# Gate and value weights of a fused mixer and two MoE layers: every chunk decoded whole in SBUF, and four low parts made on TensorE

## The chip, the cores and the metric

One core of one Trainium2 chip runs the whole program in one launch. The metric is the device time of one execution in microseconds (us); lower is better. Engines are called as in the profile: PE is TensorE, ACT is ScalarE, DVE is VectorE, POOL is GpSimd, and SP is the queue that issues the DMAs.

## The reference

A recurrent attention runs over 768 steps for 4 batches and 8 heads of 48 dimensions. Its output (3072 tokens of 384 channels) goes through a gated layer and then through a second layer:

```
for t in range(S):
    cur = einsum('bhd,bhe->bhde', u * k[t], v[t])
    y[t] = einsum('bhd,bhde->bhe', r[t], state + cur)
    state = w[t][..., None] * state + einsum('bhd,bhe->bhde', k[t], v[t])
x = y                                        # 3072 x 384
x = (sigmoid(x @ w_gate) * (x @ w_val)) @ w_out    # 384 -> 1536 -> 384
h = x @ w_in                                 # 384 -> 2048
out = (h * tanh(softplus(h))) @ w_out2       # 2048 -> 384
```

All inputs and the output are four-byte floats. The weights arrive as eight-byte integers that hold the four-byte values of two neighbours, seen by the kernel as pairs of 32-bit words.

## The kernel before, in words

**Stages.** The 768 steps are cut into 24 chunks of 32 (`NJ`), taken in 12 pairs `p` (`NP`). For every pair, `fine(p)` makes the products inside small blocks on POOL and, for pair 0, on DVE too (L487), and DVE sums them into the tile `A` (L507). `coarse(p)` transposes r, k and w of the pair on DVE (RD at L601, KD at L605, WD at L612), scales them (L624), and PE multiplies them (the scores `lp`, L643). DVE turns `A` into `X` (L653), and eight **merges** copy parts of `lp` into `X` (L664, three copies each, on ACT or DVE). `keys(p)` updates k on POOL and DVE turns it into `KT` (L696); eight **gathers** on ACT copy it into `KK` (L705). `step(j)` makes the output of a chunk on PE (`yp`, L737), splits it on ACT and DVE into a high and a low f16 part (`xs`, L213 and L216), transposes it (`xp`, L756), and copies it into `xt` (L763, L765). Then it makes the outer products for the state on PE (`kp`, L829), which read `KK`, and joins them to the state (L840).

**The two layers.** Every operand of a large matmul is held as two f16 parts, high and low, and three products are taken. For a pair `p` and each of 12 blocks `f` of 128 columns, `gate` takes nine matmuls for the gate and nine for the value (`gv`, L889), then ACT's sigmoid (L900), DVE's product (L905), ACT's high part (L917) and DVE's low part (L920) go into `gt`. `out1` multiplies `gt` by `wos` (`o`, L957). The second layer follows when all pairs are done.

**Weights of the first layer.** They come in chunks of 256 columns: six for the gate (`wg`), six for the value (`wv`), taken in turn (wg0, wv0, wg1, ...; the number in that order is `count`), then six chunks of the output weights (`wo`). Each chunk is loaded by SP (L268) and decoded: ACT takes out the spare bits (`low_`, L239) and the rebased word (`word_`, L249), DVE **joins** them by a shift and an or, ACT casts the word to f16 (the high part), and the word less the high part is the **low part**. Two ways of decoding exist:

- `decode`, for odd `count` (`WHOLE`), that is the value chunks, and for the output weights: the word lies in SBUF as one tile of 128x768; join L293 on DVE, cast L304 on ACT, low part L307 on POOL or DVE.
- `decode_early`, for even `count`, the gate chunks: the word lies in PSUM as two halves of 128x384 (in the banks `pg3` and `po`, which are free at that time); join L388 and low part L401 on DVE, twice each, and cast L398 on ACT.

**The order of the work** is set by `Plan`: every piece of work is added with its engine (or a cost for each of several engines) and with what it reads and writes, a pass from the end gives each a latest start, and a pass from the start gives every engine the ready piece whose latest start is earliest. The chosen order is then fixed for each engine's queue. Tiles with few buffers limit this order: three for raw chunks (`raw0` to `raw2`), two for words and two for spare bits (`count % 2`), two for `blk`. While pair 0 is in `gate`, its sums rotate over three PSUM banks, later over four.

## Time and profile before

| what | us |
|---|---|
| median of the three timed runs (942.68 to 943.63) | 942.82 |
| the profiled execution, its own time | 939.37 |
| span of that execution in the profile | 937.7 |
| PE busy in it | 874.2 |
| DVE, POOL, ACT busy in it | 661.3, 487.7, 479.1 |

The profile is of one execution on the one core. A line of the source (L293 and so on) is the line of the kernel before. A busy time counts an instruction from its start to its end; two neighbours on one engine overlap by some 0.08 us, so that sums of busy times are a little above the time that passes. A wait is put down to what was seen to come last.

### The profile page before, as it was taken

How to read it: one execution, taken by the hardware profiler on the slowest of the kernel's cores; microseconds unless marked ns; L12 is line 12 of the kernel's file. 1: busy time of each engine (PE TensorE's matmuls, PEld its weight loads, DVE VectorE, ACT ScalarE, POOL GpSimd, SP SyncE). 2: the span in 40 equal slices, each digit the busy share in tenths (PEclk: the TensorE clock that was granted, in tenths of full speed). 3: DMA queues.
4: the chain of work that ended last, by engine and by line, in shares of the span. 5: the costliest groups of instructions: out<-in, count | busy, mean ns of one | idle time of the engine just before them, and what ended most of it. 6: DMA issues, size and time to landing. Idle time of an engine off the chain costs nothing.

```text
span 937.7 us, 29380 instructions
## 1 busy us (share of the span) xinstructions
PE 874.2 (93%) x12808; PEld 703.9 (75%) x12808; DVE 661.3 (71%) x1094; ACT 479.1 (51%) x1065; POOL 487.7 (52%) x528
## 2 busy tenths in 40 slices
PE   0478799999999999999999999999999999999998
PEld 0366678888888888888888886667677676776788
DVE  7999985766785868677688888775655556555541
ACT  2769855352525333342528667675555655556540
POOL 8999931726565464637472275553433434334330
PEclk9989899999999999999999999999999999999999
DMA  9457742213223322232114930010200102000000
GB/s 314 135 166 227 239 119 73 60 47 81 74 60 84 83 56 72 65 85 59 53 47 119 261 102 13 12 40 2 68 1 18 52 1 69 1 19 18 1 34 35
DMA packets 56464, 71.89 MB, mean 77 GB/s; under 512 B 20752, under 2 KB 37648, under 8 KB 56208
## 3 DMA queue, kind: packets, MB, share of 16 engines
q1 hardware_dynamic: 56336, 70.03, 25.3%
q8 instruction: 100, 1.64, 0.8%
q14 instruction: 28, 0.23, 0.1%
HBM read 56.64 MB, written 9.44 MB: 70 GB/s over the span
## 4 chain that ended last, share of the span: by engine, by line
PE 78%; DVE 11%; ACT 5%; DMA 3%; issue 2%; POOL 1%; SPq 0%; ACTq 0%; DVEq 0%; POOLq 0%
PE gv L889 22%; PE h L1067 20%; PE o L1182 18%; PE o L957 13%; PE yp L737 2%; PE kp L829 2%; DVE X L664 1%; ACT X L664 1%; PE lp L643 1%; DMA raw_wp<-wo 1%; ACT KK L705 1%; DVE A L507 1%; DVE KD L605 1%; DVE WD L616 1%; DVE pt L487 1%
## 5 line engine op out<-in xcount | busy, mean ns | idle before, releaser
L1067 PE MATMUL h<-x,wis 128*128 128x512 f16 x864 | 199.9, 379 | 0.0
L889 PE MATMUL gv<-xt,wgs 128*128 128x256 f16 x1296 | 168.8, 277 | 10.5 <-DVE gt L920 7.3
L957 PE MATMUL o<-gt,wos 128*128 128x256 f16 x1296 | 166.9, 274 | 6.4 <-DVE wos L307 2.7
L889 PE MATMUL gv<-xt,wvs 128*128 128x256 f16 x1296 | 166.3, 274 | 1.3 <-DVE gt L920 0.7
L1101 POOL TENSOR_TENSOR sum<-e 128x256 f32<-128x256 f32 x96 | 71.4, 744 | 183.1 <-ACT e L1078 182.9
L487 POOL TENSOR_TENSOR blk<-blk 128x384 f32<-128x384 f32 (+3 forms) x139 | 123.6, 904 | 53.2 <-DMA blk<-rkw 33.7
L889 PEld LDWEIGHTS <-wgs 128*128 128x128 f16 x1296 | 126.5, 99 | 28.9 <-ACT X L664 6.0
L1067 PEld LDWEIGHTS <-wis 128*128 128x128 f16 x864 | 83.5, 98 | 82.9
L957 PEld LDWEIGHTS <-wos 128*128 128x128 f16 x1296 | 125.7, 98 | 25.8 <-DVE wos L307 3.4
L889 PEld LDWEIGHTS <-wvs 128*128 128x128 f16 x1296 | 126.4, 98 | 18.0 <-POOL wvs L307 1.1
L487 POOL TENSOR_TENSOR pt<-blk 128x384 f32<-128x384 f32 x93 | 107.0, 1175 | 50.3 <-DMA blk<-rkw 48.8
L1078 ACT ACTIVATE e<-h 128x512 f32<-128x512 f32 x96 | 57.3, 597 | 84.1 <-PE h L1067 83.2
L900 ACT ACTIVATE sig<-gv 128x512 f32<-128x512 f32 x72 | 43.0, 600 | 86.3 <-PE gv L889 86.0
L917 ACT CAST gt<-gv 128x512 f16<-128x512 f32 x72 | 42.0, 584 | 72.8 <-DVE gv L905 72.6
L1182 PE MATMUL o<-wps,gt 128*128 128x192 f16 x612 | 74.0, 246 | 0.0
L905 DVE SCALAR_TENSOR_TENSOR gv<-gv,sig 128x512 f32<-128x512 f32 x72 | 50.4, 702 | 25.6 <-PE gv L889 20.3
L624 POOL TENSOR_TENSOR RD<-RD,WD 128x256 f32<-128x256 f32 (+2 forms) x32 | 33.6, 1050 | 63.2 <-PE lp L643 32.9
L1120 DVE SCALAR_TENSOR_TENSOR gt<-e,gt 128x256 f16<-128x256 f32 x41 | 27.5, 682 | 49.7 <-ACT gt L1115 49.7
L920 DVE TENSOR_TENSOR gt<-gv,gt 128x512 f16<-128x512 f32 x72 | 49.3, 684 | 16.6 <-ACT gt L917 15.6
L1182 PE MATMUL o<-wps,wgs 128*128 128x192 f16 x498 | 59.4, 246 | 0.0
L664 ACT COPY X<-lp 24x64 f32<-24x64 f32 x159 | 40.7, 256 | 34.1 <-DVE X L664 25.9
L1182 PE MATMUL o<-wps,wos 128*128 128x192 f16 x456 | 57.1, 246 | 0.0
(109 smaller groups left out, 1490.4 us busy)
## 6 DMA issues: line engine op xcount, KB each, us to landing
v<-vt SPq DMA_DIRECT2D x96, 96.0 KB, 2.6
blk<-rkw SPq DMA_DIRECT2D x22, 384.0 KB, 3.8
raw_wi<-wi SPq DMA_DIRECT2D x8, 768.0 KB, 5.1
raw_wp<-wo SPq DMA_DIRECT2D x8, 768.0 KB, 5.8
blk<-rkw SPq DMA_DIRECT2D x11, 512.0 KB, 3.9
raw_wg<-wg SPq DMA_DIRECT2D x6, 768.0 KB, 6.2
raw_wv<-wv SPq DMA_DIRECT2D x6, 768.0 KB, 6.5
raw_wo<-wo SPq DMA_DIRECT2D x6, 768.0 KB, 5.4
```

Source lines behind the costliest of these rows:

```text
L487: engines[e].tensor_tensor(out=pv, in0=a, in1=b, op=ALU.mult)
L664: put(out=xp[p][o : o + t, xs, t:], in_=lps[p, e][i : i + t, :, c : c + C - t])
L889: nc.tensor.matmul(gps[p, i, o][:, h], w[:, a, kc, fs], xt[p][:, c, kc, :], start=(n == 0), stop=(n == 3 * KC - 1),)
L900: nc.scalar.activation(out=sgs[p, i], in_=gps[p, i, 0], func=AF.Sigmoid, scale=1.0 / (SW * SX))
L905: nc.vector.scalar_tensor_tensor(out=gps[p, i, 1], in0=gps[p, i, 1], scalar=SG / (SW * SX), in1=sgs.pop((p, i)), op0=ALU.mult, op1=ALU.mult,)
L917: nc.scalar.copy(out=gt[p][:, 0, 2 * i : 2 * i + 2], in_=gps[p, i, 1])
L920: nc.vector.tensor_tensor(out=gt[p][:, 1, 2 * i : 2 * i + 2], in0=gps[p, i, 1], in1=gt[p][:, 0, 2 * i : 2 * i + 2], op=ALU.subtract,)
L957: nc.tensor.matmul(ops[p, c][:, :NT], wos[:, a, f, cs], gt[p][:, g, f, :], start=(f == 0 and n == 0), stop=(f == NF1 - 1 and n == 2),)
L1067: nc.tensor.matmul(hps[r, f], w2["wi"][:, a, kc, fs], x2[r][:, c, kc, :], start=(n == 0), stop=(n == 3 * KC - 1),)
L1078: nc.scalar.activation(out=es[r, f], in_=hps[r, f], func=AF.Mish, scale=ih)
L1101: engines[e].tensor_tensor(out=sums[0][:, n - 1], in0=a(), in1=b(), op=op)
L1182: nc.tensor.matmul(ops2[h, first], home(slots[r, i, name])[:, c, tsl], w2["wp"][:, a, w, i, :], start=(new and n == 0), stop=(n == 3 * NF2 ...
```

## The change

All twelve gate and value chunks now go through `decode`, with the word whole in SBUF (`WHOLE = range(12)`). For the first four in the order (wg0, wv0, wg1, wv1; `BYPE`) the low part is made elsewhere: PE multiplies a four-byte identity (`eyes[1]`) by half of the word and adds a negative two-byte identity (`eyes[2]`) times the high part, into the PSUM banks `pg3` and `po`, and ACT casts the result to f16. POOL makes the three identities in the place of one. The weights are added to the plan step by step among the gate blocks of pair 0 (`AHEAD`), not all ahead of them, and the second transpose of r now follows the first.

```diff
--- before.py
+++ after.py
@@ -42,7 +42,9 @@
 YPOS = (4, 7)
 SEM = 0.1
 SHARED = (0,)
-WHOLE = range(1, 12, 2)
+WHOLE = range(12)
+BYPE = range(4)
+AHEAD = 2
 COLD = 1.9
 BURST = 1.42
 PARTS = ((), (0,), (1,), (2, 3))
@@ -232,6 +234,7 @@
     raws = {}
     words = {}
     lows = {}
+    rests = {}
 
     def spare_bits(key):
         low = lows[key].rearrange("p a b -> p (a b)")
@@ -269,7 +272,9 @@
 
         add("sp", 2.2, go, reads, [("raw", slot)], lat=2.0)
 
-    def decode(key, dst, n, count, slot, reads, high_on, lo_on, halves=False, blocks=None):
+    def decode(
+        key, dst, n, count, slot, reads, high_on, lo_on, halves=False, blocks=None, by_pe=False
+    ):
 
 
 
@@ -317,7 +322,26 @@
             return
         made = [[(key[0], f, a) for f in blocks or [key[1]]] for a in range(2)]
         add(high_on, 0, high, [word, *reads], made[0])
-        add(lo_on, 0, rest, [word, *made[0]], made[1])
+        if not by_pe:
+            add(lo_on, 0, rest, [word, *made[0]], made[1])
+            return
+        for h in range(2):
+            bank = (("pg", 3), "po")[h]
+            hs = slice(128 * h, 128 * h + 128)
+
+            def differ(e, h=h, hs=hs):
+                pool, tag = ((pg, "pg3"), (po, "po"))[h]
+                t = pool.tile([128, 512], F32, tag=tag, name=f"rest_{name}_{h}")
+                t = rests[key, h] = t[:, : KC * 128].rearrange("p (a b) -> p a b", a=KC)
+                nc.tensor.matmul(t, eyes[1], words[key][:, :, hs], start=True, stop=False)
+                nc.tensor.matmul(t, eyes[2], dst()[:, 0, :, hs], start=False, stop=True)
+
+            def low_part(e, h=h, hs=hs):
+                nc.scalar.copy(out=dst()[:, 1, :, hs], in_=rests.pop((key, h)))
+
+            cold = COLD if key[1] < 2 else 1.0
+            add("pe", 0.85 * cold, differ, ["eye", word, *made[0]], [bank])
+            add("act", 0.48, low_part, [bank], [made[1][h]])
 
     def combine(key, dst, word, low, reads, high_on, lo_on, count):
         sums = {}
@@ -665,7 +689,7 @@
 
         attn("dve", 1.88, flip_k, [K], [KD])
         attn("dve", 1.05, lambda e: flip_r(e, 0), [R], [(*RD, 0), (*RD, 1)])
-        attn("dve", 1.05, lambda e: flip_r(e, 1), [R], [(*RD, 2)])
+        attn("dve", 1.05, lambda e: flip_r(e, 1), [R, (*RD, 0)], [(*RD, 2)])
         attn("dve", 1.3, flip_w, [W], [WD])
         both = {"dve": 0.35, "pool": 0.65}
         attn(both, 0, lambda e: scaled(e, 5, 6, 1, 2), [WD], [(*RD, 2)])
@@ -1242,47 +1266,54 @@
     def unit(e):
 
         first = mp.tile([128, 2, NF1, NT], F16, tag="gt1", name="first")
-        eyes[0] = eye = first[:, 0, 0, :128]
-        nc.gpsimd.memset(eye, 1.0)
-        nc.gpsimd.affine_select(
-            out=eye,
-            in_=eye,
-            pattern=[[1, 128]],
-            base=0,
-            channel_multiplier=-1,
-            compare_op=ALU.is_equal,
-            fill=0.0,
-        )
+        eyes[0] = first[:, 0, 0, :128]
+        eyes[1] = first[:, 0, 1].bitcast(F32)
+        eyes[2] = first[:, 0, 0, 128:]
+        for n, value in enumerate((1.0, 1.0, -1.0)):
+            nc.gpsimd.memset(eyes[n], value)
+            nc.gpsimd.affine_select(
+                out=eyes[n],
+                in_=eyes[n],
+                pattern=[[1, 128]],
+                base=0,
+                channel_multiplier=-1,
+                compare_op=ALU.is_equal,
+                fill=0.0,
+            )
 
     add("act", 1.3, lambda e: nc.scalar.preload_act_table(AF.Sigmoid), [], ["table1"])
     add("dve", 0.2, consts, [], ["consts"])
     attn("dve", 1.3, lambda e: nc.vector.memset(A, 0.0), [], ["A"])
     halves = [("KK", i // 8, i // 4 % 2, i // 2 % 2, i % 2) for i in range(16)]
     attn("pool", 1.8, lambda e: nc.gpsimd.memset(KK, 0.0), [], halves)
-    attn("pool", 0.4, unit, [], ["eye"])
+    attn("pool", 1.5, unit, [], ["eye"])
     attn("sp", 0.1, lambda e: nc.sync.dma_start(out=U, in_=ub), [], ["U"], lat=2.0)
     load_pair(0)
     load_pair(1)
     for j in range(3):
         load_v(j)
 
-    count = 0
-    for i in range(6):
+    def weights(i):
         cs = slice(256 * i, 256 * i + 256)
-        for name, dst, w in (("wg", wgs, wg), ("wv", wvs, wv)):
+        for n, (name, dst, w) in enumerate((("wg", wgs, wg), ("wv", wvs, wv))):
+            count = 2 * i + n
             if count in WHOLE:
                 load_raw((name, i), lambda: dp, in_cols(w, cs), (KC, 256), count % 3)
                 part = lambda dst=dst, cs=cs: dst[:, :, :, cs]
                 both = [2 * i, 2 * i + 1]
-                decode((name, i), part, (KC, 256), count, count % 3, (), W1HI, W1LO, False, both)
+                by_pe = count in BYPE
+                decode(
+                    (name, i), part, (KC, 256), count, count % 3, (), W1HI, W1LO, False, both, by_pe
+                )
             else:
                 decode_early(name, i, dst, in_cols(w, cs), count)
-            count += 1
-    for i in range(6):
-        cs = slice(2 * i, 2 * i + 2)
-        dst = lambda cs=cs: wos[:, :, cs]
-        load_raw(("wo", i), lambda: dp, in_rows(wo1, cs), (2, DM), i % 3)
-        decode(("wo", i), dst, (2, DM), i, i % 3, (), W1HI, W1LO)
+        if i < 5:
+            return
+        for i in range(6):
+            cs = slice(2 * i, 2 * i + 2)
+            dst = lambda cs=cs: wos[:, :, cs]
+            load_raw(("wo", i), lambda: dp, in_rows(wo1, cs), (2, DM), i % 3)
+            decode(("wo", i), dst, (2, DM), i, i % 3, (), W1HI, W1LO)
 
     def tail1(p):
         coarse(p, cells[p])
@@ -1331,6 +1362,10 @@
             if f == 0 and p >= NP - 1:
                 load_x2(0)
                 load_x2(1)
+            if p == 0 and f % 2 == 0:
+                for i in range(AHEAD) if f == 0 else [f // 2 + AHEAD - 1]:
+                    if i < 6:
+                        weights(i)
             if f % 2 == 0:
                 fill, finish = gate(p, f // 2)
             fill(f % 2, 0)
```

Three places show how the queues move. In the names, the number behind a tile's name only tells the buffers of one program apart.

DVE at its first weights, in the middle of pair 0's transposes. Before:

```order
L605 STREAM_TRANSPOSE KD_177<-blk_95 128x32x32
L507 TENSOR_REDUCE A<-pt 128x2x4x4
L388 SCALAR_TENSOR_TENSOR word_wg_148<-word_wg_148,low_wg_143 128x384
L653 STREAM_TRANSPOSE X_257<-A 128x32x32
L401 TENSOR_TENSOR wgs<-word_wg_148,wgs 128x3x128
L664 COPY X_257<-lp_0_189 24x8x8
```

In the changed kernel:

```order
L629 STREAM_TRANSPOSE KD_176<-blk_95 128x32x32
L531 TENSOR_REDUCE A<-pt 128x2x4x4
L298 SCALAR_TENSOR_TENSOR word_wg_154<-word_wg_154,low_wg_147 128x768
L677 STREAM_TRANSPOSE X_252<-A 128x32x32
L298 SCALAR_TENSOR_TENSOR word_wv_167<-word_wv_167,low_wv_159 128x768
L688 COPY X_252<-lp_0_183 24x8x8
```

One join of 768 columns stands for the half of 384, the low part on DVE is gone, and the join of wv0 comes ahead of the merges.

DVE at the end of the decoding, where pair 2 is made ready. Before:

```order
L920 TENSOR_TENSOR gt_784<-gv_5_1_1327,gt_784 128x512
L840 TENSOR_TENSOR s_939<-kp_0_1176,s_939 128x384
L653 STREAM_TRANSPOSE X_1456<-A 128x32x32
L840 TENSOR_TENSOR s_939<-kp_1_1177,s_939 128x384
L293 SCALAR_TENSOR_TENSOR word_wo_1471<-word_wo_1471,low_wo_1432 128x768
L696 STREAM_TRANSPOSE KT<-blk_335 128x24x32
L905 SCALAR_TENSOR_TENSOR gv_0_1_1420<-gv_0_1_1420,sig 128x512
L905 SCALAR_TENSOR_TENSOR gv_1_1_1475<-gv_1_1_1475,sig 128x512
L601 STREAM_TRANSPOSE RD_1600<-blk_670 128x2x8x32
L664 COPY X_1456<-lp_0_1531 24x8x8
```

In the changed kernel:

```order
L677 STREAM_TRANSPOSE X_1558<-A 128x32x32
L298 SCALAR_TENSOR_TENSOR word_wo_1560<-word_wo_1560,low_wo_1523 128x768
L944 TENSOR_TENSOR gt_711<-gv_5_1_1322,gt_711 128x512
L688 COPY X_1558<-lp_0_1436 24x8x8
L688 COPY X_1558<-lp_0_1436 16x8x16
L688 COPY X_1558<-lp_0_1436 8x8x24
L688 COPY X_1558<-lp_0_1436 24x8x8
L688 COPY X_1558<-lp_0_1436 16x8x16
L688 COPY X_1558<-lp_0_1436 8x8x24
L864 TENSOR_TENSOR s_993<-kp_1_1248,s_993 128x384
L720 STREAM_TRANSPOSE KT<-blk_355 128x24x32
L929 SCALAR_TENSOR_TENSOR gv_0_1_1509<-gv_0_1_1509,sig 128x512
```

DVE's merges for pair 2, two of them in place of four, now come ahead of the transpose KT.

ACT at the same place. Before:

```order
L705 COPY KK<-KT 32x16x24 x2
L664 COPY X_1456<-lp_0_1531 24x8x8
L664 COPY X_1456<-lp_0_1531 16x8x16
L664 COPY X_1456<-lp_0_1531 8x8x24
L664 COPY X_1456<-lp_0_1531 24x8x8
```

In the changed kernel:

```order
L688 COPY X_1558<-lp_1_1437 24x8x8
L688 COPY X_1558<-lp_1_1437 16x8x16
L688 COPY X_1558<-lp_1_1437 8x8x24
L729 COPY KK<-KT 32x16x24
L729 COPY KK<-KT 32x16x24
L215 ACTIVATE xs_1060<-yp_0_1664 128x192
L729 COPY KK<-KT 32x16x24 x6
```

Before, two gathers stand ahead of ACT's four merges and six behind; now all eight stand behind ACT's six merges.

## Rows read from the trace of the kernel before

**Rows 1.** Busy time by stretch: each engine's us (and instructions), TensorE clock, DMA.
```profile
0.00:23.40 23.40, 0.00 (x0) 0.00 (x0) 17.70 (x22) 4.91 (x6) 18.98 (x21) 1.00 0.94 314
23.40:49.00 25.60, 13.47 (x461) 9.97 (x461) 23.80 (x40) 18.24 (x43) 24.17 (x24) 1.00 0.44 145
49.00:126.50 77.50, 60.61 (x1208) 48.21 (x1205) 72.57 (x106) 61.88 (x118) 68.54 (x59) 0.89 0.61 192
126.50:140.00 13.50, 13.47 (x292) 11.86 (x292) 13.35 (x20) 5.07 (x10) 4.66 (x6) 1.00 0.60 152
```
**Rows 2.** PE's waits from 23.4 to 126.6 us: total us, times, longest us.
```profile
PE gv L889 <- DVE gt L920: 7.3, 2, 5.9
...
PE o L957 <- DVE wos L307: 2.7, 2, 2.5
...
PE o L957 <- ACT wos L304: 1.9, 1, 1.9
```
**Rows 3.** Timeline of PE: start us, us, engine, line, out<-in, count [idle before].
```profile
48.99 2.10 PE L889 MATMUL gv<-xt,wgs 128*128 128x256 f16 x9
...
125.25 1.27 PE L829 MATMUL kp<-v,KK 32*64 32x48 f32 x60 [0.95 <-DVE xs L216]
```
**Rows 4.** Timeline of DVE and ACT where pair 2 is made ready.
```profile
112.57 2.10 DVE L696 STREAM_TRANSPOSE KT<-blk 128x768 f32<-128x768 f32 x1
116.35 0.83 ACT L664 COPY X<-lp 24x64 f32<-24x64 f32 x3 [0.52 <-PE lp L643]
119.04 1.94 DVE L664 COPY X<-lp 24x64 f32<-24x64 f32 x6 [0.90 <-ACT X L664]
...
121.86 2.07 ACT L705 COPY KK<-KT 32x384 f32<-32x384 f32 x4
123.96 0.33 ACT L213 ACTIVATE xs<-yp 128x192 f16<-128x192 f32 x1
124.31 1.03 ACT L705 COPY KK<-KT 32x384 f32<-32x384 f32 x2
```
**Rows 5.** DVE's groups, 0 to 130 us, by shape: count | busy us, mean ns | idle.
```profile
L293 DVE SCALAR_TENSOR_TENSOR word_wv<-word_wv,low_wv 128x768 uint32<-128x768 uint32 x6 | 7.3, 1219 | 0.1
L388 DVE SCALAR_TENSOR_TENSOR word_wg<-word_wg,low_wg 128x384 uint32<-128x384 uint32 x12 | 6.6, 551 | 0.3 <-ACT word_wg L249 0.3
L401 DVE TENSOR_TENSOR wgs<-word_wg,wgs 128x384 f16<-128x384 f32 x12 | 6.5, 544 | 0.0
...
L307 DVE TENSOR_TENSOR wos<-word_wo,wos 128x768 f16<-128x768 f32 x2 | 3.4, 1751 | 0.0
...
L307 DVE TENSOR_TENSOR wvs<-word_wv,wvs 128x768 f16<-128x768 f32 x1 | 1.5, 1519 | 0.0
...
L624 DVE TENSOR_TENSOR RD<-RD,WD 128x512 f32<-128x512 f32 x1 | 1.3, 1317 | 0.0
...
L624 DVE TENSOR_TENSOR RD<-RD,WD 128x768 f32<-128x768 f32 x1 | 1.0, 994 | 0.0
```
**Rows 6.** The two joins: duration ns least/median/most, first and last start.
```profile
L388 DVE SCALAR_TENSOR_TENSOR word_wg<-word_wg,low_wg x12: 541/550/566, 24.0 to 89.0; 128x384 uint32<-128x384 uint32 x12
L293 DVE SCALAR_TENSOR_TENSOR word_wv<-word_wv,low_wv x6: 966/1192/1667, 33.0 to 89.5; 128x768 uint32<-128x768 uint32 x6
```
**Rows 7.** POOL's groups, 0 to 130 us, by shape.
```profile
L809 POOL TENSOR_TENSOR s<-s,WD 128x384 f32<-128x384 f32 x10 | 10.8, 1088 | 2.1 <-DVE s L840 1.9 <-DVE s L842 0.2
L307 POOL TENSOR_TENSOR wvs<-word_wv,wvs 128x768 f16<-128x768 f32 x5 | 8.6, 1720 | 0.4 <-ACT wvs L304 0.3
...
L624 POOL TENSOR_TENSOR RD<-RD,WD 128x512 f32<-128x512 f32 x3 | 3.9, 1290 | 0.2
L624 POOL TENSOR_TENSOR RD<-RD,WD 128x768 f32<-128x768 f32 x2 | 3.0, 1484 | 2.2 <-PE lp L643 2.2
```
**Rows 8.** ACT's groups, 0 to 130 us, by shape.
```profile
L398 ACT CAST wgs<-word_wg 128x384 f16<-128x384 f32 x12 | 5.8, 480 | 8.5 <-DVE word_wg L388 8.4
...
L304 ACT CAST wvs<-word_wv 128x768 f16<-128x768 f32 x6 | 5.1, 845 | 1.2 <-DVE word_wv L293 1.2
```

## The prediction

> **What bounds the kernel.** I read first the busy time by stretch [rows 1]. Up to 23.4 us PE does nothing. From 23.4 to 49 it is busy for 13.5 of 25.6 us, from 49 to 126.5 for 60.6 of 77.5 us, and from there on it has no gap (13.47 of 13.5). In the two middle stretches DVE is busy 23.8 and 72.6 us and POOL 24.2 and 68.5 us, so these two are full, and ACT (18.2 and 61.9) has some 20% of room. All weights of the first layer are decoded before 126.5 us, so the change can only move the moment from which PE runs without a gap. What follows, some 811 us, is PE's own work, and I take it as unchanged.
>
> Next I read PE's waits in that time [rows 2]: 7.3 us for DVE's `gt`, which frees a bank of sums, and 2.7 and 1.9 us of `o` for output weights that were not yet decoded. Then I read what closes the stretch: the outer products `kp` of pair 2, which end at 125.25 + 1.27 = 126.52 us [rows 3]. Back from there [rows 4]: the last gathers on ACT end at 124.31 + 1.03 = 125.34, they stand behind ACT's merges (from 116.35), and their source KT ends on DVE at 112.57 + 2.10 = 114.67. DVE runs its queue in order with hardly a gap, so KT's time is the sum of DVE's work ahead of it. By the two PE queues the same work stands ahead of this `kp` in both kernels, but for the sixteen new matmuls. So its end can be compared straight.
>
> **The change, part by part.**
>
> *DVE's decoding.* Ahead of KT go twelve joins of 384 columns at 0.551 us and twelve low parts at 0.544 [rows 5]: 13.1 us of busy time. In come six joins of 768 columns at 1.219, two low parts of gate chunks at 1.52 (by the order, wg3 and wg4; the others go to PE and POOL) and one more low part of output weights at 1.75: 7.3 + 3.0 + 1.75 = 12.1. Neighbours overlap by 0.08, and the change has fifteen instructions fewer, so 1.2 us less of busy time is 1.0 - 1.2 = -0.2, that is, 0.2 us more of passing time.
>
> *DVE's other work.* The planner moves two scalings of RD (1.32 and 0.99) from DVE to POOL, and gives DVE a small one and one decay of the state. Neither stands in DVE's rows: half of 1.32 gives 0.66 for the first, and the low part of the same 384 elements 0.54 for the second. Net -2.31 + 1.20 = -1.1. In sum DVE loses 0.9 us ahead of KT.
>
> *The merges.* Two of DVE's merges now stand ahead of KT (the order shows it). One took 1.94 / 2 = 0.97 us, with a wait of 0.90 ahead of it [rows 4]: 1.9 to 3.7, and I take 2.7. KT then ends at 114.67 - 0.9 + 2.7 = 116.5.
>
> *ACT.* Eight new casts at the price of the half cast, 0.48, are 3.8 us, and six pairs of casts become single ones (2 x 0.480 against 0.845): -0.7 [rows 8]. These 3.1 us lie in ACT's room of 7.4 + 15.6 us [rows 1]. At the end ACT makes six merges at 0.83 and only then the eight gathers. The merges now wait for `X` and no longer for `lp`. Between the turn of `X` and KT's end DVE's order has a join, a `gt`, two merges, a state join and KT itself, some 7 us, so `X` is there at about 109.5; ACT's six merges (5.0) and DVE's two (1.9), one after the other, end at 116.5. KT and the merges are then both done at about 117. Eight gathers at 0.52 and a cast of 0.33 end at 121.5, and `kp` 1.2 us later: **122.7**, against 126.52.
>
> *PE.* Eight pairs of a four-byte and a two-byte matmul, 384 columns each. Nine matmuls of 256 columns took 2.10 us at that time of the program [rows 3], 0.23 each, so a two-byte one of 384 is 0.35 us. The four-byte one isn't in the trace: it is not below 0.35, and not above what `kp`, four-byte too, shows: 60 matmuls of 48 columns in 1.27 us, at most four side by side, make 1.8 ns a column and 0.7 us; doubled, as a safe upper end, 1.4. So a pair takes 0.7 to 1.75 us and all of them 5.6 to 14 us. I take 10. PE stands idle for 12.1 us from 23.4 to 49 and for 17 us later [rows 1], and the first gate sums may start 4 us later without harm, since the third set waits for the bank that DVE's `gt` frees (7.3 us of waits). So this costs nothing; if that cover went, it would cost up to the last pair, 1.75 us. The Trainium skill (FP8 and Floating Point Precision, TensorE Precision Notes) says that a true four-byte product takes four passes; by it and the 0.35 the pair would be at the upper end of this, which changes nothing in the sum.
>
> *POOL.* Its low parts fall from nine to eight (-1.7), one decay goes (-1.1), and two scalings come (1.29 + 1.48) [rows 7]: about nothing. The two added identities lie in the first microseconds, when POOL waits for the first block.
>
> *New waits.* Gate words now use the first word buffer, so ACT may rebase the next gate word only when the low part of the one before is done; and wv4 and wv5 wait for POOL's low parts of wv3 and wv4, which come behind other POOL work. ACT then waits, DVE's join behind it waits, and with DVE everything down to KT. Before, DVE's joins waited 0.4 us in all [rows 5]; that is the lower bound, nearly 0. Three hand-overs of a low part (1.72) with one operation ahead of it (some 1.1) are 8.5, of which some lies beside other work: the upper bound is 6. DVE's joins did find their words in time, so I stay near the lower end: 1.5.
>
> **Sum.** 126.5 - (122.7 + 1.5) = 2.3 us earlier. The profiled execution took 939.37 and would take 937.1; the median of the timed runs stands 3.45 above it, so the same step gives 942.82 - 2.3 = **940.5 us**.
>
> The stall of `o` (4.6 us) goes too, since four sets of gate sums of pair 1 now stand ahead of it. It isn't counted, because the same `kp` closes the stretch.
>
> **The rivals.**
>
> 1. *Nothing gained.* The waits for words and buffers take 2.5 to 6 us, and `kp` ends within 1.9 us of where it did. For it: DVE's total falls by 0.9 us only, and what I count as gain comes from the place of the merges. Against it: 0.4 us of such waits before. Time: 942.8.
>
> 2. *POOL and DVE get in each other's way.* The join from PSUM took 541 to 566 ns, always; the join with both inputs in SBUF took 966 to 1667 [rows 6]. So a DVE operation on two SBUF tiles waits for POOL, or POOL for it. The change puts six joins and three to five low parts more of this kind into a time when POOL never rests. The trace shows up to 0.7 us over the least for one join; nine operations at 0.4 to 0.7 on DVE, or as much on POOL, whose low parts DVE then waits for, are 4 to 6 us, and with the waits above `kp` comes 3 us later: 946. It decides from the point where POOL's low part of wv4 is later than DVE's join of wv5. Part of it is in my mean of 1.219. The Trainium skill (SBUF — State Buffer, Who interferes with whom) states it as a rule: a DVE instruction with two SBUF inputs contends with a GpSimd instruction that reads SBUF, one fully blocks, and a DVE instruction with one SBUF input doesn't contend. By that rule the spread in rows 6 is such blocking, and the trace agrees.
>
> 3. *All of PE's stalls go.* If KT isn't delayed by the merges and DVE waits for nothing, the 2.7 and 1.5 us come on top: 942.8 - 6.5 = 936.3.
>
> 4. *The change doesn't do what it says.* The four-byte matmul is far slower than its bound or its bank comes free late, the chunks 0 and 1 are ready only after 60 us, and the first `gt` with them: 4 to 6 us later, 946 to 948.
>
> **How the numbers follow.** No change, as far as a measurement can tell here, is within 0.2%, 1.9 us. The forecast has 0.40: waits of 0 to 2.5 us put it at 938.5 to 941.5, and a tenth of it lies within 0.2%. Rival 1 has 0.27, within 0.2%. Rival 2 has 0.22, three quarters and more of it slower by over 0.2% and 0.03 within. Rival 3 has 0.07, faster, and rival 4 has 0.04, slower. Faster by over 0.2%: 0.36 + 0.07 = 0.43; within: 0.04 + 0.27 + 0.03 = 0.34; slower: 0.19 + 0.04 = 0.23. The range goes from the third rival's 936.3 to just over the second's 946, 936 to 946.5. Cases of both signs hold most of the chance; the forecast's own range is 938.5 to 941.5.
>
> **What would show it.** Right: KT of pair 2 ends at 116 to 118 us, `kp` behind it at 122 to 125, the pairs on PE take 0.7 to 1.75 us and end before 54, `o` waits for no weights, the joins of the gate chunks take 1.0 to 1.7 us. The gain should be the same as the step of this `kp`. Wrong: DVE idle before joins (ACT's rebase waiting for POOL), POOL's low parts of wv3 and wv4 after 84 and 90 us, or PE idle after 126 us where it had no gap, which would mean that the start is no longer what counts.

## The result, and the profile after

The changed kernel took 953.46 us (949.43 to 954.71) where the kernel before took 942.75 beside it: 1.0121 times as long, with a 95% interval of 1.0104 to 1.0138. The forecast was 940.5 and its range ended at 946.5, so it was wrong in sign and in size. The profiled executions, 954.71 and 939.37 us, lie near the opposite ends of what each kernel's runs show, so they differ by 15.3 us where the medians differ by 10.7. What follows is told of the profiled executions unless a median is named.

The busy time of the changed kernel by stretch, for [rows 1] (length, then busy us and instructions of PE, PE's weight loads, DVE, ACT and POOL, then the granted clock, the DMA share and GB/s):

```profile
0.00:23.40 23.40, 0.98 (x85) 0.98 (x86) 17.82 (x23) 4.86 (x5) 17.30 (x23) 1.00 0.94 322
23.40:49.00 25.60, 17.58 (x352) 9.81 (x340) 22.51 (x29) 20.67 (x45) 24.96 (x23) 0.80 0.44 139
49.00:134.00 85.00, 64.14 (x1274) 52.26 (x1275) 78.39 (x97) 62.85 (x120) 76.62 (x62) 0.86 0.53 166
134.00:150.00 16.00, 12.14 (x201) 9.46 (x201) 9.39 (x14) 4.34 (x8) 2.95 (x5) 0.82 0.68 158
```

The stretch up to the end of `kp` of pair 2 is 7.5 us longer, DVE and POOL are about as full in it as before, and it isn't followed by PE without a gap any more. PE's timeline (start, duration, then line, operation, tiles, count, and in brackets the idle time ahead and what ended it) shows both:

```profile
131.03 0.37 PE L853 MATMUL kp<-v,KK 32*64 32x48 f32 x4 [1.48 <-ACT KK L729]
132.08 1.94 PE L853 MATMUL kp<-v,KK 32*64 32x48 f32 x58 [0.68 <-ACT KK L729]
134.18 2.08 PE L913 MATMUL gv<-xt,wgs 128*128 128x256 f16 x9 [0.16 <-ACT sig L924]
136.06 2.10 PE L981 MATMUL o<-gt,wos 128*128 128x256 f16 x9
...
148.07 0.28 PE L913 MATMUL gv<-xt,wvs 128*128 128x256 f16 x1 [3.70 <-issue]
```

`kp` ends at 132.08 + 1.94 = 134.02, against 126.52 [rows 3] and 122.7 + 1.5 = 124.2 in the forecast. So 9.8 of the 17.6 us by which the profiled execution missed its 937.1 are there at the end of this `kp`; the other 7.8 come behind it. Behind it nine matmuls take 2.08 us where nine of the same kind took 1.15 later in this kernel, and there is a wait of 3.70. The granted clock was at its lower level (1.2 GHz, 0.51 on the mean) from 131 to 138 us; PE had waited 1.48 us just ahead of that. The row has the columns of the first table:

```profile
131.00:138.00 7.00, 6.12 (x81) 4.71 (x82) 7.00 (x12) 6.16 (x11) 5.02 (x7) 0.51 0.33 84
```

On DVE (the timeline, for [rows 4]) KT comes 11.7 us late:

```profile
118.91 1.51 DVE L298 SCALAR_TENSOR_TENSOR word_wo<-word_wo,low_wo 128x768 uint32<-128x768 uint32 x1
120.35 0.68 DVE L944 TENSOR_TENSOR gt<-gv,gt 128x512 f16<-128x512 f32 x1
121.06 0.92 DVE L688 COPY X<-lp 24x64 f32<-24x64 f32 x3
122.87 0.96 DVE L688 COPY X<-lp 24x64 f32<-24x64 f32 x3 [0.90 <-ACT X L688]
...
124.31 2.10 DVE L720 STREAM_TRANSPOSE KT<-blk 128x768 f32<-128x768 f32 x1
```

KT ends at 126.41, against 114.67 [rows 4] and 116.5 forecast. The two merges are there and cost 2.8 us, as forecast; the queue ahead of them is what grew.

But `kp` didn't wait for KT last. Its last six gathers stand behind a cast of `xs`, which waits for PE's `yp`; and `yp` stands in PE's queue behind an `o` that waited for POOL's low part of output weights:

```profile
119.57 3.94 POOL L312 TENSOR_TENSOR wos<-word_wo,wos 128x768 f16<-128x768 f32 x2
121.97 0.39 PE L981 MATMUL o<-gt,wos 128*128 128x256 f16 x2 [2.27 <-POOL wos L312]
128.56 0.33 ACT L215 ACTIVATE xs<-yp 128x192 f16<-128x192 f32 x1 [1.07 <-PE yp L761]
128.91 3.12 ACT L729 COPY KK<-KT 32x384 f32<-32x384 f32 x6
```

From that `o` to `yp` PE has no gap. By KT alone `kp` would have ended 1.07 us earlier, at some 132.9 (an estimate from these rows), so both paths were late, POOL's a little more. In the kernel before, too, the chain into this `kp` doesn't run through KT: it runs through an `o` that waits for DVE's low parts of output weights, the scores `lp` behind it (from 115.00), the merges and `xs`:

```profile
102.61 1.46 PE L957 MATMUL o<-gt,wos 128*128 128x256 f16 x6 [2.52 <-DVE wos L307]
```

DVE's groups from 20 to 126 us in the changed kernel by shape, and POOL's two largest (for [rows 5, 7]; count, busy us, mean ns, idle before):

```profile
L298 DVE SCALAR_TENSOR_TENSOR word_wv<-word_wv,low_wv 128x768 uint32<-128x768 uint32 x6 | 10.6, 1775 | 2.9 <-ACT word_wv L252 2.8
L298 DVE SCALAR_TENSOR_TENSOR word_wg<-word_wg,low_wg 128x768 uint32<-128x768 uint32 x6 | 8.9, 1477 | 0.0
L298 DVE SCALAR_TENSOR_TENSOR word_wo<-word_wo,low_wo 128x768 uint32<-128x768 uint32 x6 | 8.8, 1483 | 0.0
...
L511 DVE TENSOR_TENSOR pt<-pt,U 128x768 f32<-128x768 f32 x3 | 5.4, 1808 | 0.0
```

```profile
L511 POOL TENSOR_TENSOR blk<-blk 128x384 f32<-128x384 f32 x27 | 33.3, 1250 | 0.4
L511 POOL TENSOR_TENSOR pt<-blk 128x384 f32<-128x384 f32 x21 | 26.9, 1307 | 0.2
```

Every one of these has two inputs in SBUF. The value joins, which the change doesn't touch, went from 1219 to 1775 ns, the gate joins came in at 1477, and POOL's products of 384 columns went from 1130 (both groups, in the profile of before) to 1250 and 1307. Lowest, median and highest of the joins, for [rows 6]:

```profile
L298 DVE SCALAR_TENSOR_TENSOR word_wg<-word_wg,low_wg x6: 1041/1336/2021, 22.9 to 90.4; 128x768 uint32<-128x768 uint32 x6
L298 DVE SCALAR_TENSOR_TENSOR word_wv<-word_wv,low_wv x6: 1374/1698/2398, 26.7 to 94.9; 128x768 uint32<-128x768 uint32 x6
```

The records show what lengthens them. However long it took, each of these twelve joins ends 0.81 to 0.82 us after a POOL instruction that ended while the join was under way. One of them, between its neighbours on POOL:

```profile
94.67 1.82 POOL L312 TENSOR_TENSOR wgs<-word_wg,wgs 128x768 f16<-128x768 f32 x1
94.91 2.40 DVE L298 SCALAR_TENSOR_TENSOR word_wv<-word_wv,low_wv 128x768 uint32<-128x768 uint32 x1
96.46 1.77 POOL L648 TENSOR_TENSOR RD<-RD,WD 128x512 f32<-128x512 f32 x1
```

POOL's low part ends at 96.49 and the join at 97.31; and POOL's scaling behind it takes 1.77 us where one of this shape took 1.06 in dependency_only (below). So the two engines take turns: beside a busy POOL such a join costs 0.82 us and what is left of POOL's instruction when it comes, and POOL's next one waits in its turn. The six value joins of the kernel before end 0.82 us after a POOL instruction too, so this was already in the spread of [rows 6].

### The profile page after: what moved, and what is told of

Read it like the earlier page. It is cut to its first block, busy times and chain, and to the rows that moved or that the text cites. A ratio compares the mean times of both kernels' runs of the same rounds, so it can differ in the third digit from the quotient of the medians.

```text
span 953.0 us, 29410 instructions
## 1 busy us (share of the span) xinstructions
PE 887.9 (93%) x12832; PEld 711.3 (75%) x12832; DVE 662.5 (70%) x1073; ACT 483.5 (51%) x1067; POOL 494.1 (52%) x531
## 4 chain that ended last, share of the span: by engine, by line
PE 85%; POOL 6%; DVE 4%; ACT 2%; issue 2%; DMA 1%; SPq 0%; POOLq 0%
PE gv L913 27%; PE h L1091 20%; PE o L1206 17%; PE o L981 15%; PE yp L761 3%; POOL pt L511 2%; PE kp L853 2%; POOL blk L511 2%; PE lp L667 1%; DMA blk<-rkw 1%; ACT X L688 1%; DVE X L688 0%; POOL s L833 0%; DVE blk L511 0%; POOL wos L312 0%
## 5 line engine op out<-in xcount | busy, mean ns | idle before, releaser
L913 PE MATMUL gv<-xt,wvs 128*128 128x256 f16 x1296 | 168.7, 276 | 8.4 <-ACT sig L924 4.3
L913 PE MATMUL gv<-xt,wgs 128*128 128x256 f16 x1296 | 170.8, 279 | 4.9 <-DVE gt L944 3.9
L511 POOL TENSOR_TENSOR blk<-blk 128x384 f32<-128x384 f32 (+2 forms) x139 | 125.1, 915 | 45.5 <-DMA blk<-rkw 35.9
L511 POOL TENSOR_TENSOR pt<-blk 128x384 f32<-128x384 f32 x93 | 110.3, 1211 | 47.6 <-DMA blk<-rkw 46.0
L648 POOL TENSOR_TENSOR RD<-RD,WD 128x512 f32<-128x512 f32 (+2 forms) x33 | 35.9, 1088 | 67.5 <-PE lp L667 31.6
```

The lines of the kernel that those rows point to most:

```text
L511: engines[e].tensor_tensor(out=pv, in0=a, in1=b, op=ALU.mult)
L913: nc.tensor.matmul(gps[p, i, o][:, h], w[:, a, kc, fs], xt[p][:, c, kc, :], start=(n == 0), stop=(n == 3 * KC - 1),)
```

## The experiments

The theories. A: two-input contention; gate joins and low parts had one operand in PSUM and now share DVE's and POOL's way to SBUF. B: the new place of the weights in the program upsets the planner's order. C: the low parts by TensorE hold something up. A fourth cause came out of the runs: the new dependency of RD's second transpose on its first, which the change brings along. A median is compared with runs of the kernel before on the same chip. All settings that aren't named stand as in the changed kernel.

**The operand's place alone.** In the kernel before, the word of a half chunk is put into SBUF; the same instructions stand in the same order on every engine.

```diff
-                pool, tag = ((pg, "pg3"), (po, "po"))[h]
-                t = pool.tile([128, 512], F32, tag=tag, name=f"word_{name}{f}")
-                words[name, f] = t[:, : KC * 128].rearrange("p (a b) -> p a b", a=KC)
+                n, tag = ((256, "word0"), (128, "half"))[h]
+                t = dp.tile([128, KC, n], F32, tag=tag, name=f"word_{name}{f}")
+                words[name, f] = t[:, :, :128]
```

> The kernel before with one edit: the words of the gate chunks' halves stand in SBUF and no longer in two PSUM banks. No engine's order of instructions changes and no instruction gets larger, so it shows the operand's place alone. Theory A (two-input contention): the twelve half joins rise from 0.55 to 0.7 to 1.1 us, the twelve half low parts from 0.54 likewise, POOL's products of 384 columns from 1.13 to 1.2 or more, KT of pair 2 ends 3 to 8 us later than 114.7, and the time is 945 to 951. Rival (the place of an operand costs nothing, the loss is the new order and the new waits): joins and low parts stay within 0.1 us, 940 to 943.

Measured: 950.77 against 940.78, ratio 1.0109 (1.0090 to 1.0129). Its spreads (lowest, median, highest), then DVE's groups and POOL's two, 20 to 126 us:

```profile
L388 DVE SCALAR_TENSOR_TENSOR word_wg<-word_wg,low_wg x12: 578/884/1342, 23.9 to 98.1; 128x384 uint32<-128x384 uint32 x12
L401 DVE TENSOR_TENSOR wgs<-word_wg,wgs x12: 531/1334/1994, 26.4 to 103.7; 128x384 f16<-128x384 f32 x12
```

```profile
L401 DVE TENSOR_TENSOR wgs<-word_wg,wgs 128x384 f16<-128x384 f32 x12 | 13.8, 1149 | 0.0
L388 DVE SCALAR_TENSOR_TENSOR word_wg<-word_wg,low_wg 128x384 uint32<-128x384 uint32 x12 | 11.2, 932 | 0.0
L293 DVE SCALAR_TENSOR_TENSOR word_wv<-word_wv,low_wv 128x768 uint32<-128x768 uint32 x6 | 8.8, 1472 | 0.0
```

```profile
L487 POOL TENSOR_TENSOR blk<-blk 128x384 f32<-128x384 f32 x27 | 33.1, 1241 | 2.0 <-DVE KD L605 1.6
L487 POOL TENSOR_TENSOR pt<-blk 128x384 f32<-128x384 f32 x21 | 26.2, 1266 | 0.2
```

The joins rose from 0.551 to 0.932 us, the low parts from 0.544 to 1.149 (11.8 us more on DVE in all), the value joins by 0.25 each, POOL's products by a tenth. All twelve joins and ten of the low parts end 0.41 to 0.42 us after a POOL instruction that ended within them; the other two low parts took 0.531 and 0.543, as from PSUM. So alone a low part costs no more, and the rest is waiting for POOL. KT ends at 125.90 and `kp` at 137.67:

```profile
123.80 2.10 DVE L696 STREAM_TRANSPOSE KT<-blk 128x768 f32<-128x768 f32 x1
```

```profile
136.40 1.27 PE L829 MATMUL kp<-v,KK 32*64 32x48 f32 x60 [0.95 <-DVE xs L216]
```

That is some 11.2 us later each, of 13.7 by which the profiled span grew; the chain into `kp` is that of the kernel before, 11.2 us later from DVE's low parts of output weights on. Theory A is shown at this order, since only the operand's place differs. The time and the joins lie in its range; KT moved further than its 3 to 8 us, and the low parts are just above 1.1. That 10.0 us here is near the 10.7 of the change proves nothing of its size there: here 24 instructions lost their PSUM operand, while in the change six joins and four low parts with two SBUF inputs come in and two such low parts go. The Trainium skill (SBUF — State Buffer, Who interferes with whom) has the rule: two SBUF inputs on DVE contend with a GpSimd instruction that reads SBUF, and one fully blocks. This run agrees, in the spread 531 to 1994 ns where the same instruction with a PSUM operand took 531 to 558.

**The change in its parts.**

```diff
-WHOLE, BYPE, AHEAD = range(12), range(4), 2
+WHOLE, BYPE, AHEAD = range(12), (), 6              # whole_only
+WHOLE, BYPE, AHEAD = range(1, 12, 2), (), 2        # order_only
+WHOLE, BYPE, AHEAD = range(1, 12, 2), (1, 3), 6    # te_low_only
+WHOLE, BYPE, AHEAD = range(12), (), 2              # whole_and_order
+WHOLE, BYPE, AHEAD = range(1, 12, 2), (), 6        # dependency_only
+WHOLE, BYPE, AHEAD = range(12), range(4), 6        # old_place
```

> All twelve gate and value chunks decoded whole, but no low parts by TensorE and the old place of the weights in the program. Theory A (two-input contention: the gate chunks' joins and low parts lost their PSUM operand and now share DVE's and POOL's way to SBUF): six gate joins of 1.4 us or more, the value joins at 1.6 or more where they took 1.22, KT of pair 2 at 120 or later, time 948 to 956. Theory B (the new place of the weights in the program order does it): no slower than before, 941 to 945. Theory C (TensorE's low parts do it): also 941 to 945.

> Even chunks in halves through PSUM as before and no low parts by TensorE; only the weights' place in the program is the new one (two pairs of chunks ahead of the first gate, one more every second gate). Theory A: gate joins at 0.55 us again, value joins near 1.22, time 941 to 945. Theory B: most of the loss is here, 948 or more, with KT of pair 2 at 120 or later. Theory C: 941 to 945.

> Only the low parts of the first two value chunks are made by TensorE and cast by ScalarE (four pairs); the gate chunks stay in halves through PSUM, the order stays the old one. Theory A: no loss, since DVE and POOL lose two low parts with two SBUF inputs: 939 to 944. Theory B: the same. Theory C (the pairs and casts hold up ScalarE and the first gate): the first gate sums start 2 us or more later and the time is 946 or more.

> The whole change but TensorE's low parts: the four low parts go back to DVE and POOL. Theory A: two-input work on DVE and POOL grows by four low parts more (1.5 us each on DVE, 1.9 on POOL), so slower than the change, 954 to 960. Theory B: like the change, 951 to 956. Theory C: back near the kernel before, 941 to 946.

> Only what the change brings beside its subject: the second scaling window of RD waits for the first, and the identities of four and two bytes are made. Chunks, low parts and place of the weights as before. If the planner's order, upset by the new dependency, is what costs: 944 to 948, and then the runs with one part alone have this in them too. If it costs nothing: 940 to 943, and each part's loss is its own.

> The whole change, TensorE's low parts included, but all weights added to the program ahead of the first gate as before. Theory A: nothing comes back, 950 to 956, gate joins at 1.4 us or more. Theory B (the new place upsets the order): 941 to 947. The run with whole chunks and no low parts by TensorE came out the same with either place, so I expect Theory A's number.

| run | median, us | before | ratio and 95% interval |
|---|---|---|---|
| whole_only | 950.69 | 941.11 | 1.0103 (1.0085 to 1.0120) |
| whole_and_order | 951.34 | 941.11 | 1.0108 (1.0092 to 1.0125) |
| order_only | 947.38 | 941.11 | 1.0072 (1.0056 to 1.0089) |
| dependency_only | 948.62 | 940.78 | 1.0083 (1.0066 to 1.0099) |
| te_low_only | 943.54 | 941.11 | 1.0027 (1.0006 to 1.0048) |
| old_place | 951.54 | 940.78 | 1.0118 (1.0098 to 1.0139) |

Three pairs of these issue the same instructions in the same order on every engine: whole_only and whole_and_order, order_only and dependency_only, old_place and the change itself. With the dependency in, the weights' place in the program moves nothing, and Theory B falls. Theory C falls as the main cause with whole_only, which has 9.6 us of the loss without TensorE's low parts; te_low_only stands 2.4 us over the kernel before, and by this table its low parts give back 4 to 5 us (against order_only and dependency_only). Theory A has a miss in whole_and_order: with four more low parts on DVE and POOL it expected 954 to 960, and got 951.34. whole_only met Theory A's time and the price of the gate joins (1.61 us), but not its path: the value joins took 1.27, and KT of pair 2 ended at 114.94, since this plan turns it earlier; its `kp` ended at 137.34 all the same, on a chain that runs through POOL's low parts of output weights. order_only (947.38) fits no theory's range; what it showed is the dependency: with it taken out again, chunks and low parts as before, the order is that of the kernel before but for the two identities. The dependency is an edge for the planner and no wait of its own, since a queue of DVE runs in order anyway. Alone it costs 6.3 and 7.8 us (the second, 948.62, is just above its expected 944 to 948). The rows of dependency_only on DVE, POOL and PE show where that begins:

```profile
19.61 1.11 DVE L625 STREAM_TRANSPOSE RD<-blk 128x512 f32<-128x512 f32 x1
20.58 1.90 DVE L629 STREAM_TRANSPOSE KD<-blk 128x1024 f32<-128x1024 f32 x1
22.34 1.07 DVE L625 STREAM_TRANSPOSE RD<-blk 128x512 f32<-128x512 f32 x1
23.27 0.27 DVE L636 STREAM_TRANSPOSE WD<-blk 128x128 f32<-128x128 f32 x1
```

```profile
27.76 1.06 POOL L648 TENSOR_TENSOR RD<-RD,WD 128x512 f32<-128x512 f32 x1
```

```profile
28.88 1.79 PE L667 MATMUL lp<-RD,KD 64*32 64x48 f32 x128 [28.88 <-POOL RD L648]
```

In the kernel before WD is turned at 18.97, POOL scales RD at 21.39 and the first scores start at 23.48. With the edge the planner puts KD and a product ahead of WD, and the first scores start 5.4 us later. The change itself doesn't show this (its first scores start before 23.4 us): with whole chunks the same edge gives another order.

**Parts without the dependency.**

```diff
-        attn("dve", 1.05, lambda e: flip_r(e, 1), [R, (*RD, 0)], [(*RD, 2)])
+        attn("dve", 1.05, lambda e: flip_r(e, 1), [R], [(*RD, 2)])
+WHOLE, BYPE, AHEAD = range(12), range(4), 2        # no_dependency
+WHOLE, BYPE, AHEAD = range(1, 12, 2), (1, 3), 6    # te_low_no_dep
+WHOLE, BYPE, AHEAD = range(12), (), 6              # whole_no_dep
```

> The whole change without the new dependency of RD's second window on its first. If that dependency upset the order and left POOL idle at 18 to 23 us: 5 us or more come back, 944 to 949. Theory A: the two-input work stays, 950 to 956.

> TensorE makes the low parts of the first two value chunks, and the new dependency of RD's second window is left out; gate chunks in halves through PSUM. The run with the dependency stood 2.4 us over the kernel before and the dependency alone 6.3 to 7.8. If parts of this kind add up, this one is 4 to 5 us faster than the kernel before, 935 to 938; if what counts is only which plan comes out, it is anywhere from 937 to 946. Theory A alone (two low parts with two SBUF inputs fewer): 938 to 941.

> All chunks whole, nothing else: no low parts by TensorE and no new dependency. Theory A: the loss of the halves whose words stood in SBUF, 10 us, less what six joins and low parts fewer save: 946 to 952, gate joins at 1.4 us or more, POOL's products of 384 columns at 1.2 or more. Rival (the dependency is what costs, the chunks nothing): 940 to 943.

| run | median, us | before | ratio and 95% interval |
|---|---|---|---|
| no_dependency | 956.20 | 940.78 | 1.0161 (1.0141 to 1.0182) |
| te_low_no_dep | 945.43 | 941.46 | 1.0040 (1.0021 to 1.0059) |
| whole_no_dep | 946.48 | 941.46 | 1.0056 (1.0036 to 1.0076) |

Whole chunks alone cost 5.0 us, within Theory A's time, though their gate joins took 1.33 us and not 1.4 or more. te_low_no_dep misses Theory A's 938 to 941 and the 935 to 938 of parts that add up; it lies where only the plan counts. The parts don't add up: the edge costs 6 to 8 us with halves, 4 to 5 with whole chunks, and taking it out of the whole change makes that 0.4% slower, beyond what I expected under either theory. TensorE's low parts give back 4 to 5 us with halves and the edge, cost some 1 us with whole chunks and the edge (old_place against whole_only), 4.0 with halves and no edge, and some 10 on top of whole_no_dep. Each edit changes what the planner puts first, and the plan's own goodness moves by several us.

**Truer prices for the planner.** It counts a join at 0.95 or 1.15 us and a low part at 1.6 or 1.85; the runs take prices nearer to the trace's.

```diff
-W1LO = {"dve": 1.6, "pool": 1.85}
+W1LO = {"dve": 1.45, "pool": 1.9}
-        full = 1.15 if key[0] == "wo" else 0.95
+        full = 1.45 if key[0] in ("wo", "wg", "wv") else 0.95
```

This is repriced; repriced_no_dep, whole_repriced_no_dep and te_low_repriced are the three kernels above with it, and before_repriced is the kernel before with it.

> The whole change, but the planner is told what the joins and low parts took in the trace: 1.45 us for a join of two SBUF inputs in place of 0.95, 1.45 and 1.9 for a low part on DVE and POOL. If the loss came from a plan made with too low prices: 5 us or more come back, 943 to 949. If it comes from the work itself, 950 to 956.

> The whole change with the planner's prices from the trace and without the new dependency. If the change's own work (two-input joins) is what is left once the plan is right: 945 to 950, like the repriced run. If all of the loss was the plan: 940 to 943.

> The kernel before with the planner's prices from the trace for the joins of two SBUF inputs and for the low parts, nothing else. If the kernel before has a plan that happens to be good and any new plan costs: 943 to 949. If truer prices make better plans in general: 937 to 940.

> All chunks whole, no low parts by TensorE, no new dependency, prices from the trace. Against the same without new prices (946.5): if prices matter, 943 or less; if the two-input work sets the time, 945 to 949.

> Gate chunks in halves through PSUM as before, low parts of the first two value chunks by TensorE, no new dependency, prices from the trace. The same without new prices took 945.4. If two low parts off DVE and POOL are worth something once the plan fits: 937 to 941. If the plan's luck decides: 942 to 948.

| run | median, us | before | ratio and 95% interval |
|---|---|---|---|
| repriced | 947.14 | 941.46 | 1.0060 (1.0038 to 1.0081) |
| repriced_no_dep | 953.70 | 941.60 | 1.0128 (1.0104 to 1.0152) |
| before_repriced | 945.60 | 941.60 | 1.0038 (1.0022 to 1.0055) |
| whole_repriced_no_dep | 949.56 | 941.60 | 1.0079 (1.0057 to 1.0102) |
| te_low_repriced | 942.80 | 941.60 | 1.0014 (0.9999 to 1.0030) |

Half of the change's loss comes back with repriced, which I first read as a plan mended by truer prices. The other runs refute that: the same prices make the kernel before 4 us slower and whole_no_dep 2 to 3; repriced_no_dep lies outside both of its expectations, and whole_repriced_no_dep just above the second of its own. New prices deal the order anew, and every new order here is slower than that of the kernel before or, with te_low_repriced (942.80, in the range for the plan's luck), can't be told from it. So the kernel before seems to have a plan at the good end, which the few orders tried here can't prove.

**Inside the change's own order.** The join only shifts the word, so that it has one SBUF input; the order is the change's on every engine.

```diff
         def join(e):
             bits = words[key].bitcast(U32)
+            if key[0] == "wg":       # all_join_one_input: in ("wg", "wv")
+                nc.vector.tensor_single_scalar(
+                    out=bits, in_=bits, scalar=3, op=ALU.logical_shift_left
+                )
+                return lows.pop(key)
```

> The change in its own order of instructions; the six gate joins only shift the word and leave out the three spare bits, so that they have one SBUF input in place of two. Theory A: these joins take one duration whatever POOL does (lowest and highest within 0.1 us, at or under the 1.04 us that was the least before), POOL's products fall from 1.25 towards 1.2, KT of pair 2 ends 3 to 6 us earlier than 126.4 and the time is 948 to 951.5. If the plan alone is late: KT within 1.5 us of 126.4, 952 to 955.

> The same for the six value joins too. Theory A: KT of pair 2 ends 7 to 12 us earlier than 126.4, time 943 to 948. If the plan alone is late: 951 to 954.

Measured: 949.88 against 941.80, ratio 1.0085 (1.0066 to 1.0104), and 947.24, ratio 1.0055 (1.0037 to 1.0074). The change stood at 1.0118 (old_place, the same order) to 1.0121, so lighter joins give back some 0.35% or 3.3 us for six, and some 6 us for twelve. KT ends at 122.59 and 121.76 in place of 126.41 (expected for the first 3 to 6 us earlier, so met; for the second 7 to 12, so missed), and POOL's products hardly changed in the first (missed). KT isn't the path, though: old_place, with the change's order, already has it at 124.42 and `kp` at 133.99. The `o` that waits for POOL's low part decides, first in gate_join_one_input, then in all_join_one_input:

```profile
119.58 0.39 PE L986 MATMUL o<-gt,wos 128*128 128x256 f16 x2 [3.24 <-POOL wos L317]
```

```profile
117.31 0.39 PE L986 MATMUL o<-gt,wos 128*128 128x256 f16 x2 [2.28 <-POOL wos L317]
```

With twelve lighter joins it starts at 117.31 in place of 121.97, and `kp` ends at 129.36 in place of 134.02: 4.66 us earlier both. With six it starts 2.39 us earlier, but the matmuls up to `yp` take 1.67 us longer, since the granted clock is at its lower level from 121 to 124 us, and `kp` ends only 0.72 us earlier; most of the gain in that run's profile lies behind `kp`, so its 3.3 us aren't shown to come by this path. Missed too is that these joins would take one duration. The spread of gate_join_one_input:

```profile
L299 DVE TENSOR_SCALAR word_wg<-word_wg x6: 555/928/1624, 22.9 to 88.7; 128x768 uint32<-128x768 uint32 x6
```

Five of the six end 0.42 us after a POOL instruction, half of the 0.82 of the join. So this form isn't free of the contention, and the 3.3 and 6 us are what a lighter join gives back, not the whole of what the second input costs.

**All chunks in halves through PSUM.**

```diff
-WHOLE = range(1, 12, 2)    # the kernel before
+WHOLE = ()
```

> The other way round: the kernel before with the value chunks too in halves whose words stand in PSUM. DVE gets twelve joins at 0.55 and twelve low parts at 0.54 (13.1 us) for six joins at 1.22 and one low part at 1.52 (8.8); POOL loses five low parts of 1.72 (8.6). Theory A: joins at 0.55, POOL's products at 1.13 or less, and between 3 us faster and 3 us slower, 938 to 944. Rival (more instructions on DVE is what counts): 945 to 950.

Measured: 950.88 against 941.46, ratio 1.0096 (1.0072 to 1.0119). The prices came as Theory A has them; the time is just above the rival's 945 to 950. Two of POOL's groups (20 to 126 us):

```profile
L487 POOL TENSOR_TENSOR blk<-blk 128x384 f32<-128x384 f32 x27 | 28.6, 1076 | 12.0 <-DVE KD L605 11.5
L487 POOL TENSOR_TENSOR pt<-blk 128x384 f32<-128x384 f32 x20 | 21.6, 1106 | 6.0 <-DMA blk<-rkw 4.6 <-DVE A L507 1.2
```

POOL's products fell to 1.08 and 1.11, all 24 half joins took 0.56 and all 24 half low parts 0.55. But the low parts that POOL made are now DVE's, and POOL stands idle for DVE's KD once for 11.5 us. It is another plan too, so it doesn't price PSUM against SBUF at one order; halves_in_sbuf does.

## Why the prediction was wrong, point by point

- **The bound.** `kp` of pair 2 as the end of the stretch in which DVE and POOL are full: right. The same PE work stands behind it in both kernels (11,144 and 11,145 matmuls from its end to the last). Hanging it on KT alone was wrong, in both kernels: the chain ran through `o`, whose stall I left out of the sum "because the same `kp` closes the stretch".
- **DVE's decoding, the step that failed.** I took six joins at the 1.219 of [rows 5] and left all other rows at their old prices. A mean read in one kernel doesn't hold in another: a join is 0.82 us and a wait for what POOL has running. Measured: gate joins 8.9 us for 7.3, value joins 10.6 for 7.3, output joins 8.8 for 8.4, two products with U 0.5 more, the decay 1.36 for 0.54; the low parts came 1.4 cheaper.
- **DVE's other work** lacks a piece: the product with U of pair 3 stands behind KT before and ahead of it in the change, 1.75 us more. With the smaller pieces, 1.2 us cheaper, DVE is busy 5.7 us longer ahead of KT than forecast. The row of before, then that of the change:

```profile
123.86 0.95 DVE L487 TENSOR_TENSOR pt<-pt,U 128x768 f32<-128x768 f32 x1
```

```profile
69.84 1.75 DVE L511 TENSOR_TENSOR pt<-pt,U 128x768 f32<-128x768 f32 x1
```

- **New waits.** Forecast 1.5, within 0 to 6. DVE waited 2.8 us for words whose rebase on ACT waited for POOL's low parts (4.8 us of ACT's waits), and 2.0 for POOL's products and others. The mechanism was right, and it cost 3.3 us more than taken. KT came 9.9 us after the 116.5 that had no such wait in it: 5.7 of work and some 4 of waits.
- **The merges** cost 2.8 (2.7 forecast).
- **ACT's room.** From KT to the end of `kp` 7.6 us, not 6.2: the cast of `xs` among the gathers waits 1.07 us for PE's `yp`, and the other six gathers stand behind it.
- **PE's pairs at nothing.** They took 12.1 us of busy time (10 taken, 5.6 to 14 the bounds) and ended before 54 us; the first gate sums start 3.7 us later, within the 4 allowed. Whether they cost nothing isn't shown: old_place and whole_only lie 1 us apart, but they differ in the place of four low parts as well.
- **POOL, about nothing:** wrong, and the other half of the step that failed. It is busy 99.0 us from 23.4 to 126.5 where it was 92.7 [rows 1], since its 48 products of 384 columns took some 7 us more. Its last low parts of output weights end at 121.9 and 123.5, where the last one ended at 115.3 before, and on the one at 121.9 hang `o` and `kp`.
- **PE unchanged after `kp`.** The work was, the time wasn't: 819.0 us in place of 811.2, of which 13.8 against 11.0 idle, and the same matmuls busy for 805.2 against 800.1. In the runs this rest lay between 810.8 and 819.0. In three profiles the granted clock never falls behind `kp` (before, te_low_only, whole_and_order), and these have the three shortest rests, 810.8 to 811.2; in the change it stands at the lower level from 131 to 138 us and again around 150. So the clock is a part of it; what sets the rest, and the wait of 3.70, which has no releaser in the profile, stay open.
- **A part that wasn't costed.** The edge on RD's second transpose is in the diff and in no step of the sum. Alone it costs 6 to 8 us.
- **The rivals.** The second (POOL and DVE in each other's way) named what happened, with 0.22 and 946; it had `kp` 3 us late, and it came 7.5 late. [rows 6] held the reason: 541 to 566 ns for 384 columns with PSUM, 966 to 1667 for 768 without. Its sentence that one SBUF input doesn't contend lacks a condition, which the last section gives. The `o` stall fell from 4.6 to 2.3 us, not to nothing, and it lay on the chain.

How the 10.7 us split between contention, plan and the rest behind `kp` isn't settled. Shown are 10.0 us for the operand's place at the order of the kernel before, some 6 us that lighter joins give back inside the change's own order, and 4 to 8 us that edges or prices without new work can cost.

## What to carry to other kernels

Where two engines share a way to SBUF, an operand in PSUM is worth more than the instruction it belongs to: price a move out of PSUM with the wait for the partner's running instruction, and raise the partner's rows too. Before a sum is hung on one wait, follow the chain back in the trace: here it left KT out. Where a greedy planner sets the order, every edge and price deals the order anew; compare the parts of a change at a frozen order, or the plan's luck is measured with them. An edit that only touches the plan belongs into the sum like any other.

## What the runs showed of the hardware that was not expected

- A shift with a single SBUF input took 555 to 1624 ns for 768 columns on DVE, so it too meets POOL's work; five of six ended 0.42 us after a POOL instruction. The Trainium skill (SBUF — State Buffer, Who interferes with whom) states that `tensor_scalar` can enter a mode that uses both ports and then contends, and that one SBUF input is free of it only outside such modes; the spread agrees.
- The kernel before took from 937.96 to 944.98 us in the runs beside the experiments. One profile against another can be off by some 5 us, and the difference of the two compared here is off by 4.6 from that of the medians.
